# One add moved to ScalarE, four small subtractions gathered on GpSimd, and a copy turned into a transfer

## The chip, the cores and the metric

The kernel runs on one core of a Trainium2 chip. The metric is device time in microseconds (us) of one execution. A profiled execution carries the profiler's record of every instruction: which engine ran it, when it began, how long it took, and what ended the idle time ahead of it. Engines are named as the profile names them: PE is TensorE (matmuls; PEld are its weight loads), DVE is VectorE, ACT is ScalarE, POOL is GpSimd, and SP is SyncE, whose queue issues most transfers. Each engine works through its own list of instructions strictly in order, and waits on semaphores for the others.

## The reference

Two layers in a row. First causal attention with 8 batches, 8 heads, 576 positions and a head size of 64, with a bias that grows with the distance:

```
scores = scale * np.matmul(q, k.transpose(0, 1, 3, 2))
bias = -(cum[:, :, :, None] - cum[:, :, None, :])
scores = np.where(causal, -1000000000.0, scores + np.minimum(bias, 0.0))
attn = np.exp(scores - max)                       # max over the row
attn = attn / (np.sum(attn, axis=-1, keepdims=True) + 1e-09)
out = np.matmul(attn, v)
```

Then a mixture of experts: each of the 4608 tokens of 512 numbers picks one of 8 experts by the largest of 8 logits, goes through that expert's two matrices with a relu between them, and is scaled by its gate. The change concerns the attention part alone; the second layer is run by code that it doesn't touch.

## The kernel before

**Pairs and steps.** Attention is done for a head of two batches at a time, a *pair*; there are 32. A pair has nine score steps, in the order 3, 7, 2, 6, 8, 1, 5, 0, 4 (`ORDER`): eight blocks of 128 query rows against 512, 384, 256 or 128 keys (the causal half), and step 8, which takes the last 64 rows of both batches against all 576 keys. `Attn.run` counts the steps of all pairs through, k = 0 to 287, and at each emits in turn: the score step, set-up work and loads, one piece of the preparation of the next pair, one piece of the oldest open tail, the transposes of the step three before (`LAG`), and background work.

**A score step** (`score`): PE makes the block of scores with two fp32r matmuls, one of the high parts of q and k (L308; L322 in step 8) and one of the low parts and the bias (L309, L323). DVE adds the mask and takes the row's maximum in one instruction (L311, L325), and ACT takes the exponential and its row sum (L331, followed by a read of the accumulator). The sums go to the tile `sums`. There are four score tiles in PSUM, so PE can run a few blocks ahead.

**The transposes** (`trans`): PE turns the exponentials (L341, L354), and ACT copies them to SBUF (L344), for step 8 DVE (L360).

**A tail** (`tail`) comes twice a pair, for g = 0 (256 rows of each batch) and g = 1 (the rest). PE multiplies the transposed exponentials by V (L381), ACT and DVE copy the result out (L384, L388), PE turns it into x with the gate's logits beside it (L275), and DVE divides: 1e-9 is added to four or five sums per row (L393), the reciprocal is taken (L394), and x is scaled (L403, L405). L393 and L394 are to be issued after `self.hold[0]`, the last score step's reduction on DVE. The division of g = 1 is emitted at place 1 of `ORDER` in the following pair (behind the reduction of score step 7), that of g = 0 at place 5 (behind that of step 1). So both stand between two score reductions in DVE's list.

**The preparation** (`prep`) of pair n+1 runs during pair n. Its inputs `rawq` and `rawk` hold each head's transposed q and k twice, in partitions 0 to 63 and again in 64 to 127. The product is made more exact by splitting each number in a rounded high part and the rest, the low part. `high` is a GpSimd multiplication by 1 that rounds to fp32r (L249), `low` a GpSimd subtraction (L253); each is chained behind the one before by `self.last`. Before the change the order is: QH twice (both batches, 128 partitions), a DVE subtraction for the low part QL of batch 0 (L259), KA twice (128 partitions), KB twice (64 partitions: the second copy of k's high part, equal to what the upper half of KA holds), the low part of k into the lower half of KA twice, and QL of batch 1. The tiles are double-buffered by pair, so a preparation can't start until PE has done the last scores of the pair before. At its head, `place` issues transfers for the bias rows of KB and QL from SP's queue (L206, L208 for the first pairs, L210, L211 later). The loads of `rawq`, `rawk` (L231) and V (L236) go through the same queue.

**Routing and experts.** After every eighth pair, `Route.group` works out the experts of 1152 tokens (small DVE operations, mostly in the last three steps of a pair), and nine GpSimd indirect transfers (L632) scatter the rows to the experts' lists, one every five or four steps. After the last pair the experts' weights are streamed in, split in high and low parts (L839 on ACT, L840 on DVE or GpSimd), and multiplied (L906, L927).

**What sets the order.** A planner puts the instructions of each engine in a list before the kernel runs. It goes through simulated time: an engine that is free takes the earliest emitted instruction whose inputs are ready by the planner's own costs. `issue_after(x)` forces an instruction behind x if both are on x's engine. The order is then fixed.

Of the kernel before, what the change touches and what calls it, by code (L numbers as in the profile page):

```python
# [7 lines left out]
F32 = mybir.dt.float32  # L8
# [3 lines left out]
AF = mybir.ActivationFunctionType  # L12
ALU = mybir.AluOpType
# [5 lines left out]
KW = 576  # L19
# [13 lines left out]
class Attn:  # L33
# [205 lines left out]
    def prep(self, pi):  # L239
        nc = self.nc  # L240
        rq, rk = self.raw.pop(pi)
        QH, QL, KA, KB = (t[pi % 2] for t in (self.QH, self.QL, self.KA, self.KB))
        QHf, KAf = QH.bitcast(F32), KA.bitcast(F32)
        if pi > 1:
            self.place(pi)

        def high(o, i):
            with self.tc.issue_after(self.last):
                self.last = nc.gpsimd.tensor_scalar(o, i, 1.0, 1.0, ALU.mult, ALU.mult).ins  # L249

        def low(o, i, h):
            with self.tc.issue_after(self.last):
                self.last = nc.gpsimd.tensor_tensor(o, i, h, ALU.subtract).ins  # L253

        lo, up = slice(0, 64), slice(64, P)
        for a in range(2):
            high(QH[:, a, :KW], rq[:, a])
        with self.tc.issue_after(self.hold[0]):
            nc.vector.tensor_tensor(QL[lo, 0, :KW], rq[lo, 0], QHf[lo, 0, :KW], ALU.subtract)  # L259
        yield  # L260
        for a in range(2):
            high(KA[:, a], rk[:, a])
        yield
        for a in range(2):
            high(KB[lo, a], rk[lo, a])
            yield
        for a in range(2):
            low(KA[lo, a], rk[lo, a], KAf[lo, a])
            yield
        low(QL[lo, 1, :KW], rq[lo, 1], QHf[lo, 1, :KW])  # L270
        yield

    def pw_(self, *a, **k):
        with self.behind():
# [87 lines left out]
    def tail(self, st, g):  # L362

        nc = self.nc
        V, PT, x, h = st["V"], st["PT"], st["x"], st["h"]
        for _ in range(TD):
            yield
        q0, q1 = (256, KW) if g else (0, 256)
        o = st["o"] if g else self.ps2.tile([P, 512], F32, name="o")
        oT = self.oT[st["pi"] % 2]  # L370

        pe, self.pe = self.pe, []
        nj = 5 if g else 2
        for j in range(nj):
            f = max(P * j, q0)
            for ab in range(2):
                r = slice(64 * ab, 64 * ab + 64)
                with ExitStack() as after:
                    for i in pe:
                        after.enter_context(self.tc.issue_after(i))  # L380
                    m = nc.tensor.matmul(o[r, f - q0:q1 - q0], V[:, ab, j, :], PT[ab][:, PTS * j + f if j < 4 else PTW - 64:PTS * j + q1 if j < 4 else PTW], start=j == 0, stop=j == nj - 1)  # L381
            pe = [m.ins]
        self.wall = m.ins
        nc.scalar.copy(oT[:, q0:q0 + 256], o[:, :256])  # L384
        if g:
            for ab in range(2):
                r = slice(64 * ab, 64 * ab + 64)
                nc.vector.tensor_copy(oT[r, 512 + 64 * ab:576 + 64 * ab], o[r, 256:320])  # L388
        yield
        n = 5 if g else 4  # L390
        rs = self.sm.tile([P, 5], F32, name="rs")
        with self.tc.issue_after(self.hold[0]):
            nc.vector.tensor_tensor(rs[:, :n], st["sums"][:, 4 * g:4 * g + n], self.eps[:, :n], ALU.add)  # L393
            nc.vector.reciprocal(rs[:, :n], rs[:, :n])  # L394
        xo = self.ps2.tile([P, 512], F32, name="ox")
        for u in range(2):
            c = 2 * g + u
            self.pw_(xo[:, 2 * XW * u:2 * XW * u + 2 * XW], oT[:, P * c:P * c + P], self.pw[:, h, :], start=True, stop=True)
        if g:
            self.pw_(xo[:, 4 * XW:5 * XW], oT[:, 512:], self.pq[:, h, :], start=True, stop=True)  # L400
        src = xo[:, :4 * XW].rearrange("p (t d) -> p t d", t=4)
        rv = rs[:, :4].unsqueeze(2).broadcast_to([P, 4, XW])
        nc.vector.tensor_tensor(x[g][:, :, :, h], src.rearrange("p t (d r) -> p t d r", r=2), rv.rearrange("p t (d r) -> p t d r", r=2), ALU.mult)  # L403
        if g:
            nc.vector.tensor_scalar(x[2][:, 0, :, h], xo[:, 4 * XW:5 * XW].rearrange("p (d r) -> p d r", r=2), rs[:, 4:5], None, ALU.mult)  # L405
        yield
# [718 lines left out]
```

## Time and profile before

| | |
|---|---|
| median of 3 runs | 902.98 us (901.18 to 905.93) |
| the profiled execution | 901.34 us, span 899.6 us |
| mean granted PE clock | 0.972 of full speed |
| busy: PE, DVE, ACT, POOL | 833.4, 640.7, 529.0, 571.3 us |
| attention | from the first score matmul at 9.4 us to about 427 us |
| experts | from about 427 us to the end |

The profile's rows give an instruction's line, engine and operation, the tiles it writes and reads, the shape, a count, busy time and mean duration, and the idle time of the engine ahead of it with what ended it. In the timeline, the first number is the start in us from the span's start, the second the duration of what is merged in the row. "PEclk" is the PE clock that was granted, as a share of full speed.

### The profile page before, as it was taken

To read this page: it belongs to the slowest core of one execution; us is meant where nothing else is said; L and a number is where in the kernel's file an instruction comes from. 1 tells how busy PE (TensorE), PEld (TensorE's weight loads), DVE (VectorE), ACT (ScalarE), POOL (GpSimd) and SP (SyncE) were. 2 spreads that over 40 slices of the span, in tenths; PEclk is the share of its full clock that TensorE was granted. 3 is DMA by queue.
4 is the path that set the end of the run, shared out by engine and by line. 5 is a ranking of instruction groups with operands and counts; after the bars stand their busy time and mean duration, and the time that the engine had idled before them with its cause. 6 is when DMAs were issued, how large, how long until landed. Compare 5 with 4: busy or idle time off the path is not lost. (4 is left out here: it accounts for less than half of the span.)

```text
span 899.6 us, 16885 instructions
## 1 busy us (share of the span) xinstructions
PE 833.4 (93%) x5648; PEld 725.2 (81%) x5648; DVE 640.7 (71%) x1540; ACT 529.0 (59%) x1226; POOL 571.3 (64%) x472
## 2 busy tenths in 40 slices
PE   3999999978999899698989899999999999999994
PEld 3878888867887778586878799999999999999962
DVE  6787787888878778876738866665655665566681
ACT  8768888766777577476634344554554544444551
POOL 9877777967788757762466355555555655455770
PEclk9999999999999889989999999999999999999997
DMA  5563544553455334334878476666666666655940
GB/s 183 154 202 120 192 141 154 193 163 101 140 180 179 119 131 140 123 118 149 304 239 305 158 281 236 237 237 237 237 236 237 238 237 237 231 222 219 330 144 3
DMA packets 68872, 172.85 MB, mean 192 GB/s; under 512 B 13231, under 2 KB 13231, under 8 KB 68656
## 3 DMA queue, kind: packets, MB, share of 16 engines
q1 hardware_dynamic: 62928, 151.70, 48.7%
q0 software_dynamic: 5856, 20.06, 5.7%
q8 instruction: 45, 0.74, 0.3%
q14 instruction: 43, 0.35, 0.1%
HBM read 144.75 MB, written 26.80 MB: 191 GB/s over the span
## 5 line engine op out<-in xcount | busy, mean ns | idle before, releaser
L331 ACT ACTIVATE pe<-pe,mx 128x512 f32<-128x512 f32 (+3 forms) x256 | 143.5, 563 | 47.1 <-DVE mx L311 45.6
L311 DVE CUSTOM_DVE_ANT_0 pe<-sp,mk 128x512 f32<-128x512 f32 (+3 forms) x256 | 121.0, 485 | 28.0 <-PE sp L309 26.1
L929 ACT ACTIVATE hT<-hp 128x512 fp32r<-128x512 f32 x72 | 42.8, 594 | 149.8 <-PE hp L927 149.8
L344 ACT COPY PT<-pt 128x512 f32<-128x512 f32 (+3 forms) x256 | 105.0, 421 | 42.9 <-PE pt L341 39.5
L308 PE MATMUL sp<-KA,QH 128*128 128x256 f32 (+2 forms) x256 | 107.8, 424 | 21.1 <-POOL KA L197 10.7
L341 PE MATMUL pt<-ident,pe 128*128 128x128 f32 x640 | 121.7, 290 | 1.8 <-ACT PT L344 1.4
L913 POOL DMA_INDIRECT out<-ys,oi x36 | 38.5, 1068 | 127.6 <-DVE ys L912 47.0
L381 PE MATMUL o<-PT,V 128*64 128x320 f32 (+4 forms) x896 | 107.7, 369 | 3.0 <-DVE PT L360 3.0
L381 PEld LDWEIGHTS o<-PT,V 128*64 128x64 f32 x896 | 78.7, 138 | 36.9 <-DVE PT L360 14.3
L249 POOL TENSOR_SCALAR QH<-rawq 128x576 fp32r<-128x576 f32 x62 | 42.2, 696 | 89.5 <-PE sp L308 85.2
L309 PE MATMUL sp<-KB,QL 76*128 76x256 f32 (+2 forms) x256 | 89.0, 350 | 2.5 <-DMA QL<-eq 2.5
L341 PEld LDWEIGHTS pt<-ident,pe 128*128 128x128 f32 x640 | 79.6, 148 | 13.5 <-issue 5.3
L253 POOL TENSOR_TENSOR KA<-rawk,KA 64x576 fp32r<-64x576 f32 x62 | 90.0, 1467 | 0.1
L927 PE MATMUL hp<-xT,wcb 128*128 128x256 f32 x648 | 89.6, 282 | 0.0
L930 DVE SCALAR_TENSOR_TENSOR hT<-hp,hT 128x512 fp32r<-128x512 f32 x72 | 49.3, 684 | 54.2 <-ACT hT L929 54.2
L927 PEld LDWEIGHTS hp<-xT,wcb 128*128 128x128 f32 x648 | 83.2, 188 | 0.6
L927 PE MATMUL hp<-xT,wcc 128*128 128x256 f32 x528 | 76.0, 284 | 5.8 <-DVE hT L930 3.1
L927 PE MATMUL hp<-xT,wca 128*128 128x256 f32 x552 | 79.1, 286 | 2.1 <-DVE hT L930 1.2
L906 PE MATMUL y<-wcb,hT 128*128 128x512 f32 x336 | 81.0, 398 | 0.0
L927 PEld LDWEIGHTS hp<-xT,wca 128*128 128x128 f32 x552 | 72.4, 191 | 3.4 <-DVE hT L930 1.4
L927 PEld LDWEIGHTS hp<-xT,wcc 128*128 128x128 f32 x528 | 69.2, 192 | 6.8 <-DVE hT L930 3.3
L906 PEld LDWEIGHTS y<-wcb,hT 128*128 128x128 f32 x336 | 62.8, 188 | 14.7
(267 smaller groups left out, 1957.7 us busy)
## 6 DMA issues: line engine op xcount, KB each, us to landing
wrbw<-in_w SPq DMA_DIRECT2D x104, 512.0 KB
wraw<-in_w SPq DMA_DIRECT2D x56, 512.0 KB
rawq<-in_qkv SPq DMA_DIRECT2D x32, 576.0 KB
rawk<-in_qkv SPq DMA_DIRECT2D x32, 576.0 KB
xg<-lists SPq DMA_DIRECT2D x18, 576.0 KB
V<-in_qkv SPq DMA_DIRECT2D x32, 320.0 KB
lists<-z SPq DMA_DIRECT2D x8, 576.0 KB
ekd<-ek SPq DMA_DIRECT2D x2, 720.0 KB
```

Of the source, the lines that this page charges most:

```text
L253: self.last = nc.gpsimd.tensor_tensor(o, i, h, ALU.subtract).ins
L308: self.pe.append(nc.tensor.matmul(sp[:, :nn], QH[:, q0:q0 + P], KA[:, ab, :nn], start=True, stop=False).ins)
L309: self.pe.append(nc.tensor.matmul(sp[:, :nn], QL[:EXT, q0:q0 + P], KB[:EXT, ab, :nn], start=False, stop=True).ins)
L311: ins = nc.vector.tensor_tensor_reduce(out=t[:, :n], in0=sp[:, :n], in1=self.mk[:, 512 - n:512], scale=-0.125, scalar=3.0e38, op0=ALU.add, ...
L331: self.act = nc.scalar.activation(t[:, :n], t[:, :n], AF.Exp, bias=m, scale=-1.0, accum_out=st["sums"][:, o:o + 1]).ins
L341: self.pe.append(nc.tensor.transpose(out=pt[:, P * j:P * j + P], in_=pe[:, P * j:P * j + P], identity=self.ident).ins)
L344: cp(w[:, :, v:v + P], pt[:, :P * (c + 1)].rearrange("p (j q) -> p j q", q=P))
L381: m = nc.tensor.matmul(o[r, f - q0:q1 - q0], V[:, ab, j, :], PT[ab][:, PTS * j + f if j < 4 else PTW - 64:PTS * j + q1 if j < 4 else PTW], ...
L906: self.last[0] = nc.tensor.matmul(y[u], hT[:, a, f, P * u:P * u + P], W[4 + f // 2][:, c, 512 * (f % 2):512 * (f % 2) + 512], start=f == 0 ...
L927: nc.tensor.matmul(hp[:, u], W[k][:, a, f:f + P], xT[:, c, k], start=k == 0 and i == 0, stop=k == 3 and i == 2)
L929: nc.scalar.activation(hs, hp, AF.Relu)
L930: nc.vector.scalar_tensor_tensor(hT[:, 1, 2 * m:2 * m + 2], hp, 0.0, hs.bitcast(F32), ALU.max, ALU.subtract)
```

## The change

Three edits in two functions.

1. In `tail`, the 1e-9 is added by ACT (an Identity activation with the constant as its bias) instead of by DVE. The new instruction is to be issued after the last exponential on ACT (`self.act`) as the tail is emitted, the reciprocal after the last reduction on DVE, as before. The reciprocal waits for ACT now.
2. In `prep`, QL of batch 0 is made by GpSimd too; DVE has no part in the preparation any more.
3. In `prep`, KB is no longer made by two GpSimd multiplications, but by two transfers from SP's queue that copy the upper half of KA to the lower half of KB (64 partitions x 576 numbers each, 144 KB). The order becomes: KA twice, the two transfers, QH twice, QL twice, the low part of KA twice.

```
@@ prep
         lo, up = slice(0, 64), slice(64, P)
         for a in range(2):
-            high(QH[:, a, :KW], rq[:, a])
-        with self.tc.issue_after(self.hold[0]):
-            nc.vector.tensor_tensor(QL[lo, 0, :KW], rq[lo, 0], QHf[lo, 0, :KW], ALU.subtract)
+            high(KA[:, a], rk[:, a])
+        for a in range(2):
+            nc.sync.dma_start(KB.bitcast(F32)[lo, a], KAf[up, a])
         yield
         for a in range(2):
-            high(KA[:, a], rk[:, a])
+            high(QH[:, a, :KW], rq[:, a])
         yield
         for a in range(2):
-            high(KB[lo, a], rk[lo, a])
+            low(QL[lo, a, :KW], rq[lo, a], QHf[lo, a, :KW])
             yield
         for a in range(2):
             low(KA[lo, a], rk[lo, a], KAf[lo, a])
             yield
-        low(QL[lo, 1, :KW], rq[lo, 1], QHf[lo, 1, :KW])
-        yield
@@ tail
-        with self.tc.issue_after(self.hold[0]):
-            nc.vector.tensor_tensor(rs[:, :n], st["sums"][:, 4 * g:4 * g + n], self.eps[:, :n], ALU.add)
+        with self.tc.issue_after(self.hold[0]), self.tc.issue_after(self.act):
+            nc.scalar.activation(rs[:, :n], st["sums"][:, 4 * g:4 * g + n], AF.Identity, bias=self.eps[:, :1])
             nc.vector.reciprocal(rs[:, :n], rs[:, :n])
```

## The prediction

> **What bounds the kernel now.** I cut the attention at starts of the GpSimd preparation, one per pair, and asked for busy time and granted clock by stretch: five pairs from 94.3 us in which nothing is scattered, then the three stretches (five, five and two pairs) in which L632 scatters rows. Columns: stretch, length, then busy us (instructions) of PE, PEld, DVE, ACT, POOL, then the granted PE clock.
>
> ```profile
> 94.30:150.40 56.10, 56.05 (x447) 49.08 (x446) 45.32 (x185) 45.18 (x146) 42.53 (x46) 1.00 0.45 151
> 150.40:217.70 67.30, 59.36 (x437) 50.47 (x436) 55.33 (x174) 45.19 (x142) 51.52 (x54) 0.97 0.52 171
> ...
> 251.60:320.70 69.10, 61.83 (x438) 52.29 (x436) 54.47 (x176) 45.70 (x142) 51.80 (x55) 0.92 0.50 166
> ...
> 355.70:391.00 35.30, 27.24 (x176) 22.82 (x175) 30.32 (x86) 18.24 (x58) 22.07 (x24) 0.85 0.44 155
> ```
>
> In the first stretch PE is busy 56.05 of 56.10 us: a quiet pair takes 56.1 / 5 = 11.2 us and PE sets it. The other three do as many pairs' matmuls, but are longer than 11.2 us a pair by 67.3 - 56.0 = 11.3, 69.1 - 56.0 = 13.1 and 35.3 - 22.4 = 12.9 us, 37.3 us together. PE idles there, and its clock falls. The groups of instructions and one such pair in the timeline say why:
>
> ```profile
> L253 POOL TENSOR_TENSOR KA<-rawk,KA 64x576 fp32r<-64x576 f32 x62 | 90.0, 1467 | 0.1
> ...
> L393 DVE TENSOR_TENSOR rs<-sums,eps 128x5 f32<-128x5 f32 x64 | 49.8, 778 | 1.8 <-ACT pe L331 1.8
> ...
> L249 POOL TENSOR_SCALAR KB<-rawk 64x576 fp32r<-64x576 f32 x62 | 47.4, 777 | 0.2
> ...
> L253 POOL TENSOR_TENSOR QL<-rawq,QH 64x576 fp32r<-64x576 f32 x31 | 43.9, 1416 | 0.1
> ...
> L259 DVE TENSOR_TENSOR QL<-rawq,QH 64x576 fp32r<-64x576 f32 x31 | 31.4, 1011 | 0.0
> ```
>
> ```profile
> 208.33 2.81 POOL L253 TENSOR_TENSOR KA<-rawk,KA 64x576 fp32r<-64x576 f32 x2
> ...
> 208.78 3.75 DVE L393 TENSOR_TENSOR rs<-sums,eps 128x5 f32<-128x5 f32 x1
> ...
> 211.11 1.40 POOL L253 TENSOR_TENSOR QL<-rawq,QH 64x576 fp32r<-64x576 f32 x1
> ...
> 212.56 0.19 DVE L394 RECIPROCAL rs<-rs 128x5 f32<-128x5 f32 x1
> ...
> 214.04 0.39 PE L308 MATMUL sp<-KA,QH 128*128 128x256 f32 x1 [1.48 <-DVE mx L311]
> ```
>
> L393 adds five numbers per partition, and takes 0.16 us when it is alone (the row at 104.11 below), but 0.78 us in the mean. Here it takes 3.75 us: it begins during a GpSimd subtraction and ends at 212.53, 0.02 us behind the end of the last of three such subtractions in a row (211.11 + 1.40). The reciprocal behind it, with one input, takes its 0.19 us. So a DVE add with two SBUF inputs is held up while GpSimd subtracts. The score reductions stand behind it in DVE's list, and PE runs out of score tiles: 1.48 us of idle at 214.04. In scatter pairs the scatters push the subtractions to where L393 comes; in quiet pairs they mostly miss.
>
> At this place a page of the skill can be weighed. The Trainium skill, page "SBUF — State Buffer", section "Who interferes with whom", says that DVE and GpSimd share a pair of ports, and that the one that comes second is blocked until the first finishes its instruction. The trace agrees on who is blocked, but not on how long: 3.75 us is more than two subtractions of 1.4. What the page's length would make of the time is the last rival below.
>
> **The change, part by part.** Base: the profiled execution's own 901.34 us (span 899.6 and 1.7 around it); the median of the runs is 902.98, 1.6 higher, and I leave that aside.
>
> *The add leaves DVE: the stall goes.* With the subtraction L259 gone as well, no DVE instruction of an ordinary pair has two SBUF inputs against GpSimd's. I take back all of the excess in the first two scatter stretches, 11.3 + 13.1 = 24.4 us, the lower clock with it, since it falls behind PE's idle. In the third, another small DVE instruction with two SBUF inputs stalls too, and it stays:
>
> ```profile
> 378.14 3.32 DVE L728 SCALAR_TENSOR_TENSOR fbase<-fex,fs 128x6 f32<-128x6 f32 x1
> ```
>
> There I take half, 6.4 of 12.9 us. Two more L393 meet the weights' GpSimd work as attention drains,
>
> ```profile
> 412.94 2.15 DVE L393 TENSOR_TENSOR rs<-sums,eps 128x4 f32<-128x4 f32 x1
> ...
> 420.49 2.02 DVE L393 TENSOR_TENSOR rs<-sums,eps 128x4 f32<-128x4 f32 x1 [1.76 <-ACT pe L331]
> ```
>
> of whose 4.2 us I count half, 2. Gain: 24.4 + 6.4 + 2 = 33 us (28 if the drain and a part of the third stretch give nothing, 40 if all comes back).
>
> *The add arrives on ACT: a new wait.* Around the division of g = 0 in a quiet pair:
>
> ```profile
> 104.11 0.16 DVE L393 TENSOR_TENSOR rs<-sums,eps 128x4 f32<-128x4 f32 x1
> ...
> 104.31 0.18 DVE L394 RECIPROCAL rs<-rs 128x4 f32<-128x4 f32 x1
> ...
> 104.45 0.52 ACT L331 ACTIVATE pe<-pe,mx 128x256 f32<-128x256 f32 x1
> 104.50 0.28 PE L309 MATMUL sp<-KB,QL 76*128 76x256 f32 x1
> 104.59 0.46 DVE L403 TENSOR_TENSOR x<-ox,rs 128x288 f32<-128x288 f32 x1
> ...
> 104.86 0.19 ACT L331 ACTIVATION_READ_ACCUMULATOR pe<-pe,mx 128x1 f32 x1
> ...
> 104.95 0.85 ACT L344 COPY PT<-pt 128x384 f32<-128x384 f32 x2
> 104.96 0.41 DVE L311 CUSTOM_DVE_ANT_0 pe<-sp,mk 128x256 f32<-128x256 f32 x1
> ...
> 105.44 0.29 DVE L311 CUSTOM_DVE_ANT_0 pe<-sp,mk 128x128 f32<-128x128 f32 x1
> ...
> 105.48 0.66 PE L354 MATMUL pt<-ident,pep 128*128 128x128 f32 x4
> ...
> 105.65 0.34 DVE L360 COPY PT<-o 64x64 f32<-64x64 f32 x2
> ...
> 106.17 0.76 DVE L360 COPY PT<-pt 128x256 f32<-128x256 f32 x2 [0.18 <-PE pt L354]
> 106.19 0.40 ACT L331 ACTIVATE pe<-pe,mx 128x128 f32<-128x128 f32 x1
> ...
> 106.88 2.37 PE L381 MATMUL o<-PT,V 128*64 128x320 f32 x20
> ```
>
> The new ACT instruction stands behind the exponential of 104.45, so it can't start before 105.05 (104.86 + 0.19). Its price has no row, so bounds: an ACT copy of 128x8 takes 0.19 us (L623, below), the same kind of activation on 128 columns 0.40. From 256 to 128 columns it falls by 0.12 us; another 0.11 less for the last 123 columns makes 0.29, which I take. It fires the reciprocal at about 105.4, against 104.31 now. What does DVE do meanwhile? The score block of 104.50 is done at 104.78, so a planner that looks for what is ready takes its reduction first (0.41, to about 105.3), then reciprocal and scaling (0.18 + 0.46, to 106.0), the reduction of 105.44 (0.29), and the copies L360 (0.34 + 0.76): they end at about 107.4 instead of 106.93, and PE's L381 waits for them. So some 0.45 us of bubble per pair, where PE has none to spare. The ACT copies of 104.95 come 0.29 later, and the transposes of 105.48, which take the PSUM tile that the first copy frees, with them; that lies beside the same 0.45. At g = 1 DVE's next reductions are ready sooner than the sums, and nothing of PE's hangs on the scaling. 32 pairs x 0.45 = 14.4 us. Bounds per pair: 0, if reciprocal and scaling are put behind L360; 1.15, if the planner puts the reciprocal right behind its reduction and DVE stands still until 105.4 (L360 ends 0.9 later), with 0.25 us from the second ACT instruction. I take 0.45, since the planner goes by what is ready.
>
> ```profile
> L83 ACT ACT_TABLE_LOAD x1 | 1.3, 1283 | 0.8 <-PEq L1110 0.8
> ...
> L623 ACT COPY x<-tok 128x8 f32<-128x8 f32 x8 | 1.2, 191 | 0.0
> ```
>
> Only one table load stands in the whole trace, though Identity (L107) and Exp both run behind it: no reloading.
>
> *GpSimd.* It gains one subtraction per pair (1.42) and loses two multiplications (2 x 0.78 = 1.55): level. Does it become the bound where it scatters as well?
>
> ```profile
> 150.37 1.33 POOL L249 TENSOR_SCALAR QH<-rawq 128x576 fp32r<-128x576 f32 x2 [3.16 <-PE sp L308]
> ...
> 160.13 1.42 POOL L253 TENSOR_TENSOR QL<-rawq,QH 64x576 fp32r<-64x576 f32 x1
> ```
>
> With two scatters inside, a preparation runs from 150.37 to 161.55, 11.2 us, as long as a quiet pair; it begins a little ahead of its pair (it waited 3.16 us for PE), so PE is just not kept waiting. I count 0, with up to 0.3 us for each of the 12 scatter pairs as the bound (4 us). The four subtractions are now in one row.
>
> *The transfers.* KB is fed from KA, 1.3 us into the preparation, and is needed when the next pair begins, about 10 us later.
>
> ```profile
> L206 SPq DMA_DIRECT2D KB<-ek x32: 653/720/1173, 11.1 to 86.1; - x32
> ```
>
> ```profile
> SPq L231 <- POOL KA L253: 79.7, 11, 8.6
> ```
>
> The SBUF-to-SBUF transfers of now take SP 0.72 us each to issue (median); two more per pair fit in a queue that is otherwise waiting. Cover: 10 us. They stand behind `place` and wait for GpSimd's multiplication; behind them stand the loads of rawq, rawk and V, which already wait up to 8.6 us for GpSimd and are used a pair later. Cost 0; if a load that waits for the last subtraction came ahead of them in the queue, they would be issued 7 us later and could land a microsecond late in each pair.
>
> **Sum:** 901.3 - 33 + 14.4 = 882.7, so 883 us; its own range, with 28 to 40 for the gain and 0.2 to 0.8 us per pair for the new wait, is 867 to 899, most likely 874 to 892.
>
> **The rivals.** (a) *The new wait hides*: the planner puts reciprocal and scaling where DVE would idle. For it: DVE is busy 45.3 of 56.1 us in quiet pairs. Against: the copies L360 come right after. 901.3 - 33 = 868. (b) *The reciprocal blocks DVE*: put right behind its reduction at both tails, 1.15 us a pair, 36.8 us: 901.3 - 33 + 36.8 = 905, slower than before. It decides from 33 / 32 = 1.03 us a pair. For it: in the rows above, add, reciprocal and scaling follow their reduction directly. Against: then they were ready. (c) *The lock finds others*: four subtractions in a row hold DVE up to 4 x 1.42 = 5.7 us, and the routing has small DVE adds with two SBUF inputs, like L728. One such stall for each of three groups: 883 + 17 = 900. Against: L728 is the only routing add of the attention part that takes over 1 us in the trace of before. (d) *KB comes late*, 1 us in each pair: 883 + 32 = 915. Against: the 10 us of cover. (e) *A wait lasts one GpSimd instruction at most, and the rest has another cause that stays*: of the 3.6 us that the L393 of 208.78 takes too long, one subtraction's 1.4 comes back, 40%; of the gain 0.4 x 33 = 13 us: 901.3 - 13 + 14.4 = 903. Against: the wait shown ends with the last of three subtractions, not with the first. The rule of the Trainium skill quoted above, "SBUF — State Buffer", "Who interferes with whom", speaks for it.
>
> **How the numbers follow.** Forecast 0.52, (a) 0.22, (b) 0.12, (c) 0.06, (d) 0.05, (e) 0.03. A change under 0.5% of 902.98, 4.5 us, can't be told from none, so faster means under 898.5 and slower over 907.5. Faster: nearly all of the forecast, (a), half of (c), 0.76. Slower: (d) and nearly half of (b), 0.10. The rest, 0.14, is no change. The range of 8 in 10 takes the forecast and (a) and stops ahead of (b): 862 to 901.
>
> **What would show it.** Right: no L393 on DVE, the reciprocal still at 0.19 us, PE's clock at 1.00 through 150 to 350 us, scatter pairs as long as quiet ones, and quiet pairs at 11.4 to 12.0 us with PE waiting for L360. Wrong: quiet pairs at 11.2 (a) or above 12.2 us with DVE idle ahead of L394 for ACT (b); a routing add on DVE of 4 us or more (c); PE waiting for a DMA into KB at L309 (d); stretches that stay over 60 us although no L393 is left (e).

## The result, and the profile after

The changed kernel takes 878.22 us in the median of 4 runs (874.9 to 884.02), beside 904.45 us of the kernel before on the same chip; the ratio is 0.9709, with a 95% interval of 0.9633 to 0.9785. It is faster by 26 us. The forecast was 883 us, range 862 to 901.

The profiled execution took 879.26 us, span 877.5 us, against 901.34 and 899.6 before: 22.1 us of span. The first table cuts attention at the first score matmul of a pair, in the same way for both kernels: four quiet pairs, the five pairs of the first scatter stretch, the five of the second, the two of the third (shown for the changed kernel alone), and the drain up to the first expert matmul. Columns as in the prediction (length, then busy us of PE, PEld, DVE, ACT, POOL, then the granted PE clock). First the kernel before:

```profile
95.10:139.60 44.50, 44.50 (x352) 39.04 (x350) 36.41 (x147) 35.95 (x116) 34.09 (x37) 1.00 0.47 158
151.20:218.60 67.40, 59.46 (x439) 50.58 (x437) 55.26 (x173) 45.29 (x143) 51.62 (x55) 0.97 0.51 166
252.50:322.40 69.90, 62.63 (x438) 53.13 (x436) 54.42 (x172) 45.85 (x143) 52.60 (x56) 0.91 0.48 159
...
404.00:428.10 24.10, 21.19 (x140) 15.41 (x138) 16.52 (x50) 15.90 (x45) 5.08 (x3) 0.93 0.47 159
```

and the changed kernel:

```profile
94.00:139.70 45.70, 45.17 (x351) 38.46 (x349) 31.03 (x135) 37.49 (x122) 32.63 (x33) 1.00 0.52 164
152.60:209.30 56.70, 56.21 (x434) 47.31 (x432) 36.52 (x156) 46.17 (x150) 49.68 (x49) 1.00 0.70 214
245.10:302.30 57.20, 56.25 (x434) 47.36 (x433) 37.05 (x156) 46.20 (x150) 49.52 (x50) 1.00 0.66 198
338.20:367.80 29.60, 24.00 (x173) 19.31 (x171) 24.35 (x77) 18.34 (x60) 20.97 (x21) 0.94 0.56 172
...
379.20:402.00 22.80, 20.13 (x145) 15.45 (x144) 13.27 (x51) 17.28 (x51) 5.88 (x4) 1.00 0.42 150
```

The two long scatter stretches shrink by 10.7 and 12.7 us, and PE is busy in 56.2 of their 57 us at full clock: a scatter pair is now as long as a quiet one. The third shrinks by 5.7 us (35.3 in the prediction's cut, which has the same length here, 29.6 now), the drain by 1.3. The four quiet pairs grow by 1.2 us, 0.3 each: 11.1 us before, 11.4 now. The first expert matmul comes at 402.0 instead of 428.1 us, 26.1 earlier; the experts' part then takes 877.5 - 402.0 = 475.5 us instead of 899.6 - 428.1 = 471.5, so 4.0 us are given back there.

The groups of ACT and DVE that hold the division:

```profile
L391 ACT ACTIVATE rs<-sums,eps 128x5 f32<-128x5 f32 x64 | 18.3, 288 | 0.0
```

```profile
L392 DVE RECIPROCAL rs<-rs 128x5 f32<-128x5 f32 x64 | 11.5, 180 | 3.1 <-ACT rs L391 2.8
```

The add costs ACT 0.288 us. The reciprocal is at 0.18 us, and DVE stood idle ahead of it for ACT for 2.8 us in 64 divisions. PE never waited for KB: the one DMA wait of the matmuls that read it (L307) is 2.4 us for a constant of the start.

Around the division of g = 0 in a quiet pair, in time order (start, duration):

```profile
105.06 0.18 DVE L392 RECIPROCAL rs<-rs 128x4 f32<-128x4 f32 x1
...
105.23 0.29 DVE L309 CUSTOM_DVE_ANT_0 pe<-sp,mk 128x128 f32<-128x128 f32 x1
...
105.44 0.45 DVE L401 TENSOR_TENSOR x<-ox,rs 128x288 f32<-128x288 f32 x1
...
106.26 0.76 DVE L358 COPY PT<-pt 128x256 f32<-128x256 f32 x2
```

This is nearly the order on DVE that the prediction gave: reciprocal, scaling, the copies L358. Only the score reduction of 105.23, which the prediction had behind the scaling, stands ahead of it. ACT's add runs from 104.75 to 105.04, and DVE doesn't stand idle ahead of the reciprocal.

Rival (c) is there too, once in attention. The routing's subtraction L722 begins during a scatter and ends behind the fourth subtraction of the row:

```profile
352.22 1.03 POOL L630 DMA_INDIRECT lists<-x,di  x1 [0.16 <-issue]
352.60 6.18 DVE L722 TENSOR_TENSOR fs<-numf,fs 128x6 f32<-128x6 f32 x1
353.29 2.77 POOL L253 TENSOR_TENSOR QL<-rawq,QH 64x576 fp32r<-64x576 f32 x2
...
356.01 2.74 POOL L253 TENSOR_TENSOR KA<-rawk,KA 64x576 fp32r<-64x576 f32 x2
...
359.81 0.49 PE L273 MATMUL ox<-pq,oT 128*128 128x72 f32 x1 [4.75 <-DVE oT L386]
```

353.29 + 2.77 and 356.01 + 2.74 are the four subtractions; L722 ends at 358.78, 0.03 us behind the last. PE stands 4.75 us; this is most of what is left over 22.8 us (two pairs of 11.4) in the third stretch. The same picture costs time among the experts:

```profile
424.47 0.96 POOL L630 DMA_INDIRECT lists<-xq,di  x1 [0.30 <-issue]
424.82 8.74 DVE L838 TENSOR_TENSOR wcc<-wraw,wcc 128x1024 fp32r<-128x1024 f32 x1 [5.28 <-ACT wcc L837]
425.46 2.41 POOL L838 TENSOR_TENSOR wca<-wrbw,wca 128x1024 fp32r<-128x1024 f32 x1
...
430.13 2.33 POOL L838 TENSOR_TENSOR wcc<-wraw,wcc 128x1024 fp32r<-128x1024 f32 x1
...
433.61 0.79 PE L925 MATMUL hp<-xT,wcc 128*128 128x256 f32 x2 [5.30 <-DVE wcc L838]
```

A weight subtraction on DVE, begun during the last scatter, is held through three subtractions of GpSimd, and PE waits 5.30 us for its tile.

### The profile page after: what moved, and what is told of

It is laid out like the page before. It is cut to its first block, busy times and chain, and to the rows that moved or that the text cites. A ratio compares the mean times of both kernels' runs of the same rounds, so it can differ in the third digit from the quotient of the medians.

```text
span 877.5 us, 16898 instructions
## 1 busy us (share of the span) xinstructions
PE 823.0 (94%) x5648; PEld 712.4 (81%) x5648; DVE 580.5 (66%) x1445; ACT 540.5 (62%) x1290; POOL 555.8 (63%) x441
## 5 line engine op out<-in xcount | busy, mean ns | idle before, releaser
L342 ACT COPY PT<-pt 128x512 f32<-128x512 f32 (+3 forms) x256 | 106.7, 417 | 36.4 <-PE pt L339 32.9
L339 PE MATMUL pt<-ident,pe 128*128 128x128 f32 x640 | 119.7, 286 | 1.4 <-ACT PT L342 1.2
L379 PE MATMUL o<-PT,V 128*64 128x320 f32 (+4 forms) x896 | 108.7, 364 | 5.3 <-DVE PT L358 5.3
L306 PE MATMUL sp<-KA,QH 128*128 128x256 f32 (+2 forms) x256 | 101.2, 403 | 11.3 <-POOL KA L197 10.8
L379 PEld LDWEIGHTS o<-PT,V 128*64 128x64 f32 x896 | 72.2, 136 | 41.5 <-DVE PT L358 12.3
L249 POOL TENSOR_SCALAR KA<-rawk 128x576 fp32r<-128x576 f32 x62 | 41.7, 689 | 78.3 <-PE sp L306 57.2
L339 PEld LDWEIGHTS pt<-ident,pe 128*128 128x128 f32 x640 | 76.3, 145 | 17.3 <-ACT PT L342 7.3
L307 PE MATMUL sp<-KB,QL 76*128 76x256 f32 (+2 forms) x256 | 86.7, 341 | 2.4 <-DMA QL<-eq 2.4
L253 POOL TENSOR_TENSOR KA<-rawk,KA 64x576 fp32r<-64x576 f32 x62 | 87.0, 1420 | 0.1
L253 POOL TENSOR_TENSOR QL<-rawq,QH 64x576 fp32r<-64x576 f32 x62 | 86.5, 1411 | 0.2
```

The source lines that it names most:

```text
L306: self.pe.append(nc.tensor.matmul(sp[:, :nn], QH[:, q0:q0 + P], KA[:, ab, :nn], start=True, stop=False).ins)
L307: self.pe.append(nc.tensor.matmul(sp[:, :nn], QL[:EXT, q0:q0 + P], KB[:EXT, ab, :nn], start=False, stop=True).ins)
L339: self.pe.append(nc.tensor.transpose(out=pt[:, P * j:P * j + P], in_=pe[:, P * j:P * j + P], identity=self.ident).ins)
L342: cp(w[:, :, v:v + P], pt[:, :P * (c + 1)].rearrange("p (j q) -> p j q", q=P))
```

## The experiments

Theory 1: the DVE add, held by GpSimd's subtractions, was the cost, and moving it away is the gain. Its rival, theory 2: the gain comes from a lighter preparation. A second question is what the new wait costs, a third how long GpSimd holds DVE. Line numbers shift by a few from kernel to kernel, and `[...]` in a cut of code stands for the slice of four or five sums. Each ratio is to the kernel before on the same chip. The runs were spread over several chips, so a few microseconds between two changed kernels mean little by themselves.

**Edit 1 alone.** The kernel before, with only the add moved:

```
 # tail; prep as before
-            nc.vector.tensor_tensor(rs[:, :n], st["sums"][...], self.eps[:, :n], ALU.add)
+            nc.scalar.activation(rs[:, :n], st["sums"][...], AF.Identity, bias=self.eps[:, :1])
```

> The kernel before with one edit alone: the add of 1e-9 on ScalarE. GpSimd's preparation, DVE's subtraction L259 and the six multiplications stay as before. Theory 1 (the add with two SBUF inputs, held up by GpSimd's subtractions, was the cost): scatter pairs fall from 13.5 to 18.1 us to 11.4 to 12.5 us, no half clock between 200 and 320 us, time 876 to 888 us; DVE's remaining subtraction L259 may stretch beyond its 1.01 us where it meets GpSimd, at up to 1.4 us each. Theory 2 (the gain comes from the lighter preparation: no subtraction on DVE, no second multiplication of k): scatter pairs stay at 13.5 us and more, time 897 to 905 us.

Measured: 893.43 us (892.33 to 896.19), ratio 0.9894 (0.9869 to 0.9919): 11 us faster, less than half of the change, and between the ranges of the two theories. One pair in each of the two long scatter stretches still takes 16.6 us, now because of the preparation's subtraction on DVE. The first of them:

```profile
180.32 1.06 POOL L632 DMA_INDIRECT lists<-x,di  x1 [0.17 <-issue]
181.41 1.32 POOL L249 TENSOR_SCALAR KA<-rawk 128x576 fp32r<-128x576 f32 x2
181.43 5.88 DVE L259 TENSOR_TENSOR QL<-rawq,QH 64x576 fp32r<-64x576 f32 x1
...
183.96 2.74 POOL L253 TENSOR_TENSOR KA<-rawk,KA 64x576 fp32r<-64x576 f32 x2
```

L259, 1.01 us in the mean before, takes 5.88 us: it is held through four multiplications of GpSimd (two each at 181.41 and 182.69) as well as two subtractions; so multiplications with one input hold it too. The long hold has only moved to the next DVE instruction with two SBUF inputs.

**Edits 2 and 3 alone.** The new preparation, with the add still on DVE:

```
 # prep as after; tail as before
+            low(QL[lo, a, :KW], rq[lo, a], QHf[lo, a, :KW])       # both a on GpSimd
             nc.vector.tensor_tensor(rs[:, :n], st["sums"][...], self.eps[:, :n], ALU.add)
```

> The changed kernel's preparation (four subtractions on GpSimd in a row, KB by transfers) with the add still on DVE with two SBUF inputs. Theory 1 (the add is what GpSimd holds up): the four subtractions in a row now hold the add for up to 5.7 us, the pairs in which it meets them take 13 to 18 us, PE's clock falls to a half in more windows than before; time 895 to 930 us, no faster than before. Theory 2 (the lighter preparation made the gain): 868 to 880 us, pairs of 11.1 to 11.4 us.

Measured: 926.51 us (923.47 to 930.29), ratio 1.0264 (1.0235 to 1.0292): 22 us slower. Theory 2 falls. With -11 and +22 apart and -26 together, the parts are not additive: each edit takes one of DVE's two victims away, and only both leave none. Two adds of this run, the first in a quiet pair, the second in a scatter pair:

```profile
99.97 2.81 POOL L253 TENSOR_TENSOR QL<-rawq,QH 64x576 fp32r<-64x576 f32 x2
101.83 0.97 DVE L391 TENSOR_TENSOR rs<-sums,eps 128x5 f32<-128x5 f32 x1
102.72 2.81 POOL L253 TENSOR_TENSOR KA<-rawk,KA 64x576 fp32r<-64x576 f32 x2
...
184.15 1.06 POOL L630 DMA_INDIRECT lists<-x,di  x1 [0.17 <-ACT pe L329]
...
186.53 2.79 POOL L253 TENSOR_TENSOR QL<-rawq,QH 64x576 fp32r<-64x576 f32 x2
188.10 4.00 DVE L391 TENSOR_TENSOR rs<-sums,eps 128x5 f32<-128x5 f32 x1
189.28 2.78 POOL L253 TENSOR_TENSOR KA<-rawk,KA 64x576 fp32r<-64x576 f32 x2
```

Both adds begin during the second of four subtractions in a row. The first ends at 102.80, 0.02 us behind that subtraction (99.97 + 2.81): one instruction was waited for, though two more followed at once. The second ends at 192.10, behind the fourth.

**Does a scatter make the difference?** In the kernel of the last experiment, the first group's nine scatters give way to GpSimd multiplications:

```
+            if bp == 0:
+                for _ in range(2):
+                    nc.gpsimd.tensor_scalar(un, xr[:, :512], 1.0, 1.0, ALU.mult, ALU.mult)
+            else:
                 i = nc.gpsimd.indirect_dma_start(out=self.lists, ...)
```

> The kernel with the new preparation and the add on DVE (e2), but the nine scatters of the first group are replaced at their place by two GpSimd multiplications on 128x512 each; the rows of the first group never reach the lists, zero rows are written there at the start instead, so the outputs of that group's tokens are left out. The scatters of the other groups stay and serve as control. Its total time is not to be compared. Theory 1 (behind a scatter GpSimd keeps the port over several instructions; without one DVE gets it at the next boundary): in the first group (about 150 to 220 us) no add takes more than 1.5 us, pairs of 11.4 to 12.0 us; in the second group adds of 2.7 to 4.3 us, pairs of 15 to 17 us, as in e2. Theory 2 (any back-to-back row of GpSimd instructions holds DVE to its end): adds of 2.7 to 4.3 us in the first group too.

Measured (one execution; its total says nothing): the first group has no add over 1.33 us, the second has 3.99, 3.14 and 4.05 us. One add of the first group, then one of the second:

```profile
213.57 1.42 POOL L253 TENSOR_TENSOR KA<-rawk,KA 64x576 fp32r<-64x576 f32 x1
213.71 1.30 DVE L391 TENSOR_TENSOR rs<-sums,eps 128x5 f32<-128x5 f32 x1
214.96 0.61 POOL L639 TENSOR_SCALAR un<-x 128x512 f32<-128x512 f32 x1
...
316.54 1.06 POOL L641 DMA_INDIRECT lists<-x,di  x1 [0.17 <-ACT pe L329]
...
320.49 3.99 DVE L391 TENSOR_TENSOR rs<-sums,eps 128x5 f32<-128x5 f32 x1
321.68 2.78 POOL L253 TENSOR_TENSOR KA<-rawk,KA 64x576 fp32r<-64x576 f32 x2
```

At 213.71 GpSimd's next multiplication stands ready behind the running subtraction and begins as soon as that ends (214.96), and the add still gets in at the boundary. The nearest scatter's end is 2.9 us ahead of the add of 320.49. The pairs of the first group take 11.1 to 11.9 us. Theory 1 holds for these adds: without a scatter a hold lasts to the end of the running instruction, behind one it can last through the whole row. That it isn't the whole rule, the run without the transfers shows below.

**Does one input suffice to be held?** The add back on DVE, with 1e-9 as a constant:

```
-            nc.scalar.activation(rs[:, :n], st["sums"][...], AF.Identity, bias=self.eps[:, :1])
+            nc.vector.tensor_scalar(rs[:, :n], st["sums"][...], 1.0e-9, None, ALU.add)
```

> The changed kernel with the add back on DVE, but with one input from SBUF and 1e-9 as a constant of the instruction. Theory 1 (only a DVE operation with two SBUF inputs is held by GpSimd's subtractions): the add takes 0.15 to 0.2 us everywhere, pairs of 11.1 us, 868 to 872 us, faster than the changed kernel. Theory 2 (a one-input add on DVE is held as well, as the 128x9 operation of the routing, 1.0 us in the changed kernel against 0.16 before, lets one think): adds of 1 to 5 us in the scatter pairs, half clock between 150 and 350 us, 885 to 925 us.

Measured: 926.5 us (923.37 to 929.5), ratio 1.0231 (1.0191 to 1.0272), as slow as with two inputs. The groups:

```profile
L391 DVE TENSOR_SCALAR rs<-sums 128x5 f32<-128x5 f32 x64 | 65.2, 1018 | 1.4 <-ACT pe L329 1.4
L392 DVE RECIPROCAL rs<-rs 128x5 f32<-128x5 f32 x64 | 11.7, 183 | 2.1
```

Theory 1 of this run, which was also the prediction's wording ("two SBUF inputs"), falls: the one-input TENSOR_SCALAR from SBUF to SBUF takes 1.018 us in the mean and up to 4.35 (at 385.11), the RECIPROCAL right behind it 0.183 us. What is held depends on the operation, not on the number of inputs alone. The Trainium skill, page "SBUF — State Buffer", section "Who interferes with whom", names both DVE operations with two SBUF inputs and those in a two-port mode as contending with GpSimd. The mean of 1.018 us here agrees with that if the TENSOR_SCALAR ran in such a mode, which no run shows; the reciprocal, at 0.183 us, was not held.

**What does the new wait cost?** First without any add:

```
-            nc.scalar.activation(rs[:, :n], st["sums"][...], AF.Identity, bias=self.eps[:, :1])
-            nc.vector.reciprocal(rs[:, :n], rs[:, :n])
+            nc.vector.reciprocal(rs[:, :n], st["sums"][...])
```

> The changed kernel with no add at all: the reciprocal reads the sums directly, so 1e-9 is left out of every division. It prices the whole of the new wait. If ScalarE's add costs the 0.3 us per pair by which a pair of the changed kernel (11.4 us) is longer than a quiet pair before (11.1): pairs of 11.1 us and 878 - 32 x 0.3 = 868 us. If the 0.3 us comes from elsewhere (the preparation's new order, the transfers): pairs stay at 11.4 us and the time at 876 to 880 us.

Measured: 871.55 us (869.76 to 872.05), ratio 0.9636 (0.9617 to 0.9655). Against the changed kernel's 878.22 that is 6.7 us, 0.2 us per pair. The intervals of the two ratios overlap a little, but every run here is faster than every run of the changed kernel (874.9 us and more), and the undisturbed pairs take 10.9 to 11.0 us, as the first theory has it. By stretches (five, five and two scatter pairs):

```profile
152.00:207.70 55.70, 55.64 (x441) 46.24 (x441) 36.87 (x159) 45.41 (x143) 50.94 (x50) 1.00 0.71 224
242.40:298.40 56.00, 55.76 (x444) 46.33 (x442) 37.39 (x160) 45.63 (x144) 50.33 (x50) 1.00 0.66 204
333.10:364.30 31.20, 24.78 (x183) 20.71 (x181) 26.26 (x85) 18.92 (x60) 21.66 (x23) 0.95 0.53 165
```

This is the first step of the prediction by itself: 67.4 - 55.7 = 11.7 and 69.9 - 56.0 = 13.9 us come back in the long stretches.

Then with the add kept on ACT, but unread:

```
+            nc.scalar.activation(un[:, :n], st["sums"][...], AF.Identity, bias=self.eps[:, :1])
+            nc.vector.reciprocal(rs[:, :n], st["sums"][...])
```

> The changed kernel with ScalarE's add kept at its place but written to a tile that nobody reads; the reciprocal reads the sums directly, so 1e-9 is left out of every division. It splits the price of the add. If the 0.3 us per pair is DVE's waiting chain (add, reciprocal, scaling, copies L358): pairs of 11.1 us, 868 us, and PE's waits for ScalarE's copies L342 gone. If it is ScalarE's time (0.29 us ahead of the copies L342): pairs of 11.4 us, 878 us, and the waits of PE's transposes for L342 stay at about 6 us in 28 instructions.

Measured: 877.66 us (874.15 to 878.12), ratio 0.9695 (0.9671 to 0.9718), the changed kernel's time. This run didn't settle it: quiet pairs are at 11.1 to 11.2 us, as the first theory has it, but three other pairs of every eight take 11.8 to 12.5, because the planner orders them otherwise, and the total is the second theory's. PE's waits for ACT's copies L342 are nearly gone, as the first theory has it: between 94 and 340 us its weight loads wait 0.4 us in 2 of them, against 4.1 us in 22 in the changed kernel.

So the add was issued early instead, at the start of the division's chain:

```
     def tail(self, st, g):
+        with self.tc.issue_after(self.act):
+            nc.scalar.activation(rs[:, :n], st["sums"][...], AF.Identity, bias=self.eps[:, :1])
         ...
-            nc.scalar.activation(rs[:, :n], st["sums"][...], AF.Identity, bias=self.eps[:, :1])
             nc.vector.reciprocal(rs[:, :n], rs[:, :n])
```

> The changed kernel with ScalarE's add issued at the start of the division's chain, as soon as the sums are there, instead of directly ahead of the reciprocal. ScalarE's work is the same, DVE need not wait. Theory 1 (DVE's wait costs): pairs of 11.1 to 11.2 us, 868 to 872 us. Theory 2 (ScalarE's 0.29 us ahead of its copies L342 cost, wherever they stand): 876 to 879 us.

Measured: 880.65 us (879.46 to 881.74), ratio 0.9722 (0.9687 to 0.9756), by its total nearer to theory 2. The stretches say otherwise (the second and the third scatter stretch):

```profile
244.30:300.90 56.60, 56.18 (x442) 48.23 (x440) 37.91 (x159) 46.22 (x153) 50.07 (x50) 1.00 0.67 204
335.30:373.20 37.90, 28.18 (x180) 23.40 (x179) 30.98 (x85) 19.44 (x63) 21.11 (x22) 0.86 0.45 135
```

Undisturbed pairs take 11.1 us again, and the second stretch is 0.6 us shorter than the changed kernel's; without the add it is 1.2 shorter. So in these stretches about half of the add's price is its place. The other half stays when it stands early, and also when nobody reads its result (quiet pairs of 11.1 to 11.2 against 10.9 to 11.0 us), which points to ACT's own time. The third stretch is 8.3 us longer: two routing operations are held over rows of subtractions, 4.77 and 6.19 us long, each begun during a scatter. Where they meet such a row is the luck of the planner's order.

**The routing's stall.** One step of a pair earlier:

```
-QUIET = (6, 7, 8)
+QUIET = (5, 6, 7)
```

> The changed kernel with the routing's small DVE operations placed one step of a pair earlier (steps 5, 6, 7 of 9 in place of 6, 7, 8). Theory 1 (the pair of 18.1 us is only the routing's subtraction L722, 6.18 us beside four subtractions of GpSimd): where it misses them that pair takes 11.4 to 12.9 us and the time falls by 5 to 7 us to 871 to 873 us; where it meets them at the new place too, nothing changes. Theory 2 (that pair is long for another reason, the third group's end): it stays above 17 us with L722 under 1 us.

Measured: 876.16 us (871.52 to 878.76), ratio 0.9663 (0.9622 to 0.9705); against the changed kernel's interval this can't be told apart. L722 misses the row, but the conversion behind it (a one-input CAST, 128x6) meets it with 4.20 us, and that pair takes 16.1 instead of 18.1 us.

**The transfers.** KB by GpSimd again:

```
-            nc.sync.dma_start(KB.bitcast(F32)[lo, a], KAf[up, a])
+            high(KB[lo, a], rk[lo, a])
```

> The changed kernel with KB made by GpSimd's multiplications again in place of the two transfers; four subtractions in a row and ScalarE's add stay. GpSimd then has 2 x 0.78 = 1.55 us more in each pair. Theory 1 (GpSimd has no room left: its preparation with two scatters inside would take 11.2 + 1.5 = 12.7 us against a pair of 11.4): the 12 scatter pairs take 12.5 us or more, quiet pairs 11.4 us, time 890 to 905 us, so the transfers are a part of the gain. Theory 2 (the transfers matter to nothing, the gain lies in what DVE no longer does): 876 to 881 us.

Measured: 890.29 us (888.44 to 893.53), ratio 0.9835 (0.9786 to 0.9884), 12 us slower than the changed kernel: theory 1's total, but not by its mechanism.

```profile
248.10:305.30 57.20, 56.24 (x434) 47.36 (x432) 37.03 (x156) 46.19 (x150) 55.40 (x58) 1.00 0.52 166
342.00:381.00 39.00, 27.45 (x173) 22.11 (x172) 30.62 (x78) 18.51 (x60) 23.51 (x26) 0.78 0.36 118
```

GpSimd is busy 55.4 of 57.2 us, and scatter pairs still take 11.4 us: it isn't the bound even there. Most of the loss is in the third stretch, 39.0 against 29.6 us, where two routing operations are held (6.18 and 4.65 us). Three pairs in which nothing is scattered take 12.4 instead of 11.4 us. In each of them a small routing subtraction, 0.23 us when it is alone, takes 1.5 us; the first:

```profile
130.02 1.30 POOL L249 TENSOR_SCALAR KB<-rawk 64x576 fp32r<-64x576 f32 x2
130.52 1.52 DVE L590 TENSOR_TENSOR lg<-lg,rmx 128x72 f32<-128x72 f32 x1
131.29 1.30 POOL L249 TENSOR_SCALAR QH<-rawq 128x576 fp32r<-128x576 f32 x2
```

L590 begins during the first of these four multiplications and ends at 132.04, behind the third, although the first scatter is still to come. So a hold over several instructions is possible without a scatter as well; what makes the difference there stays open.

**A version that beats both.** The early add, with the routing's first table on GpSimd instead of DVE, so that little of it can be held:

```
+        ve = nc.gpsimd if tag == "f" else nc.vector
-        nc.vector.tensor_tensor(oh, oh, a, ALU.mult)
+        ve.tensor_tensor(oh, oh, a, ALU.mult)
...
-        nc.vector.tensor_tensor(s, bf, s, ALU.subtract)
+        nc.gpsimd.tensor_tensor(s, bf, s, ALU.subtract)
```

(likewise the picks' products, the scaling, the base and the two conversions of that table).

> The changed kernel with ScalarE's add issued early (e9), and the routing's small products, subtraction and conversions of its first table (L670, L678, L723 to L728 and the two conversions) on GpSimd in place of DVE. Theory 1 (pairs of e9 at 11.1 us, and its two pairs of 18.9 and 19.0 us are DVE's routing operations held by GpSimd): those two pairs fall to 11.4 to 13.5 us, time 864 to 870 us. Theory 2 (they are long for another reason, or GpSimd's small operations are slow enough to delay its preparation): 878 to 885 us.

Measured: 867.67 us (865.62 to 870.56), ratio 0.9593 (0.9568 to 0.9618), 10.5 us below the changed kernel, and the two intervals don't meet. Theory 1 holds. The third stretch, and one of the moved operations:

```profile
333.50:358.50 25.00, 23.09 (x180) 19.53 (x179) 18.78 (x77) 18.65 (x64) 22.78 (x30) 1.00 0.61 193
```

```profile
348.73 0.20 POOL L725 TENSOR_TENSOR fs<-numf,fs 128x6 f32<-128x6 f32 x1
```

37.9 us have become 25.0; what cost DVE 6 us of holding costs GpSimd 0.20. On the kernel without the add, the same edit:

> The same edit of the routing on the kernel without the add (e3; 1e-9 is left out of every division). Theory 1: the pair of 18.2 us of e3 falls to 11.4 to 13.0 us, time 871.5 - 6 = 864 to 867 us. Theory 2: 870 to 874 us.

Measured: 866.27 us (863.65 to 867.78), ratio 0.9572 (0.9546 to 0.9599), as theory 1 said. Its interval overlaps that of the version before, so with early issue and a clean routing the add's price can no longer be told from nothing.

## Why the prediction was right, point by point

**The stall goes (33 us): right.** No DVE instruction with two SBUF inputs is left in ordinary pairs. Without the add, the two long stretches give 11.7 + 13.9 = 25.6 us (forecast 24.4), the third 35.3 - 31.2 = 4.1 (forecast 6.4), and the whole kernel 904.6 - 871.6 = 33 us. That these hang on the preparation's subtraction as much as on the add was in the step, in one clause ("with the subtraction L259 gone as well"); the run with edit 1 alone shows that more than half hangs on such clauses: -11 us instead of -26. The reason that the step gave for the scatter pairs (the scatters push the subtractions to where the add comes) isn't enough: with the first group's scatters taken away the adds there still met GpSimd's instructions, but were held for 1.10 to 1.31 us only. The scatter also makes the hold longer.

**The new wait (14.4 us): the mechanism half right, the size too large by a factor of two.** The order on DVE came nearly as written, but the term measured 6.7 us by the run without the add, 0.2 per pair instead of 0.45 (0.3 by the quiet pairs), inside the bounds of 0 to 1.15. The prediction laid it on the copies L358 being late for PE's L379. But those waits didn't grow. The waits that grew are those for ACT's copies, which the step named too and counted as lying beside the first. PE's weight loads by what they waited for (us, times, longest), the kernel before and then the changed one:

```profile
PEld o L381 <- DVE PT L360: 14.3, 31, 1.7
PEld pt L341 <- ACT PT L344: 2.5, 4, 1.4
```

```profile
PEld o L379 <- DVE PT L358: 12.3, 31, 1.6
PEld pt L339 <- ACT PT L342: 7.3, 31, 1.4
```

How the 0.2 us divides exactly stays open: early issue takes back about half.

**GpSimd level (0) and the transfers (0): right in ordinary pairs.** The run without the transfers, in which GpSimd is busy 1.2 us more per pair (55.4 against 49.5 us in five), still has scatter pairs of 11.4 us. The 12 us which the transfers are worth in total come for the most part through the routing's holds, which no step priced.

**Rivals.** (a) and (b) did not come: pairs grew by 0.3 us, between their 0 and 1.15. (c) came once in attention at 6.18 us, near its 5.7, while the L728 of before fell away. The same hold cost 5.30 us of PE's time among the experts, where PE's waits for these tiles (wcc) were 2.8 us before; that is 2.5 of the 4.0 us given back there, which the sum left out. The other part isn't explained: without the add, where those waits are 2.9 us, the experts' part still takes 473.4 us, 1.9 more than before. So the sum was 883 for 879.3 of the profiled execution because the wait was about 8 us too high and the experts 4 us too low. That the two errors partly cancel is luck. (d) did not come. (e) was dismissed with a row that holds for scatter pairs only: in the run with edits 2 and 3 alone the adds of the quiet pairs waited for one GpSimd instruction (0.97 to 1.33 us); nearly all of the longer holds have a scatter just ahead. In this kernel the gain sits in the scatter pairs, so its 903 us was wrong all the same.

**What would show it.** PE's clock is 1.00 in both long stretches, scatter pairs are as long as quiet ones, the reciprocal is at 0.18 us, quiet pairs are at the low end of 11.4 to 12.0. "PE waiting for L360" came, but no more than before, so it was no sign of the new wait; and the sign of (c), a routing operation of 4 us or more, came once in attention.

## What to carry to other kernels

Where a tiny DVE operation is 20 times too long, look at what GpSimd does beside it, and at every DVE operation of that kind at once: taking one away moves the hold to the next (one edit gave -11 us, the other +22, both -26). Move such an operation to an engine that GpSimd didn't hold (ACT's add took 0.31 us at most in every kernel that has it) and issue it where its input is ready, not where its result is needed; or give it to GpSimd itself, where six numbers per partition cost 0.20 us. After each such change read the stretches again, since a new order of the list meets the row at another place: the third stretch took 29.6, 37.9 and 39.0 us in three kernels, for the most part for this reason.

## What the runs showed of the hardware

**Behind a scatter, GpSimd can keep DVE out over a whole row.** In a row of four subtractions without a gap an add was let in after one (0.97 us), or after all (4.00 us). In the traces of before and of the runs with edit 1 alone, with edits 2 and 3 alone and with the one-input add, every hold of attention over three or more GpSimd compute instructions began during a scatter or less than 3 us behind the end of one; farther from one, holds crossed one or two. With the first group's scatters taken away its adds took 1.33 us at most. It is no strict rule. In the kernel before, L726 at 377.47, 0.5 us behind a scatter, was let in after the running multiplication (0.63 us), while L728 right behind it was held through three instructions (3.32 us). In the run without the transfers, L590 was held through three multiplications in three pairs, 18 us or more from the last scatter or ahead of the first. Why a scatter has this effect (its transfer that is still running, or something else that GpSimd does for it) was not tried.

**Held and not held.** On DVE from SBUF to SBUF, the two-input TENSOR_TENSOR, the one-input TENSOR_SCALAR and the converting CAST were held, up to 8.74 (a large one, 128x1024), 4.35 and 4.20 us; the RECIPROCAL took 0.16 to 0.22 us in every kernel, also where it began while GpSimd was multiplying or subtracting.

**GpSimd nearly full isn't GpSimd bound.** At 55.4 busy of 57.2 us it kept PE waiting in no ordinary pair.
